# Converting the second MoE's weights two pieces a step, with four more pieces converted in the first MoE's last two steps

## The chip, the cores and the metric

One NeuronCore of a Trainium2 chip runs the whole program. The metric is the device time of one execution in microseconds (us). Engine names are those of the profile: PE is TensorE's matmul, PEld its weight load, DVE is VectorE, ACT is ScalarE, POOL is GpSimd, SP is SyncE, whose queue issues the DMAs.

## The reference

Three layers follow each other, all in float32.

```
attention: 4 batches x 8 heads, 512 local tokens (window of 32 each side) and 32 global ones, head size 64
x    = attention output, rearranged to (2304 tokens, 512)
MoE1: h = x @ w_in (512x1024); s = h * softmax(h); ln = (s - mean) / sqrt(var + 1e-6) * g_ln; x = ln @ w_out (1024x512)
MoE2: h = x @ w_in (512x2048); g = h where h >= 1, 0 where h <= -1, else (h + 1)^2 / 4; out = g @ w_out (2048x512)
```

Weights reach the kernel as 64-bit words (float64 numbers), so every weight has to be turned into float32 on the chip before a matmul can use it.

## The kernel before, in words

**Precision.** Each float32 operand is held as a pair (hi, lo) of fp32r tiles: `split` (L124) lets ACT copy the value to hi, and DVE or POOL subtracts hi from it to give lo. A product is three matmuls (hi by hi, hi by lo, lo by hi), written by `mm3` (L175).

**Weights.** A piece is a [128, 512] block of weights, 512 KB as 64-bit words. `fetch` (L159) issues its DMA into a raw buffer, and `convert` (L129) makes hi and lo of it: ACT takes the absolute value of the high words (L137), DVE does four passes (clamp L139, shift L143, sign L145, low bits L147), and `split` writes hi (ACT) and lo (DVE or POOL). A pair of pieces goes through these passes side by side. The raw buffers (tag `wraw`) are three and the working tiles (tag `w32`) are three. A raw buffer comes free when L147 has read its low words, and only then does SP issue the next load into it; `weights(n)` (L167) converts the next n pieces, and the `fetch` behind it tops the prefetched pieces up to three.

**Pieces and stages.** Sixteen pieces belong to MoE1. `CONV` and the first four entries of `STEP` (1, 2, 3, 2) use them up, so the list of pieces to do is empty from then until entry 12. The 32 pieces of MoE2 come in the order of `order2` (L449): for each 128 columns f of the 2048, its w_in piece ("i", f) and, two later, its w_out piece ("o", f). Counted from 0, piece 2f - 2 is thus ("i", f) for f from 2 on, and piece 2f + 3 is ("o", f) for f up to 13.

MoE1 runs in 17 steps p, one for each tile of 128 tokens (L597). A step multiplies tile p by w_in (`b1`), then does a layer-norm chain on DVE, ACT and POOL, transposes the tile of the step before (`b3`), and multiplies by w_out (`b4`). From step 12 on each step converts `STEP[p]` pieces of MoE2: 1, 2, 2, 1, 1, seven in all, with POOL doing the lo subtraction.

MoE2 runs over three blocks of tokens b (6, 6 and 5 tiles) and, within a block, over the 16 column groups f, one "step" of the loop at L660 each. A step converts pieces (with DVE doing the lo subtraction), multiplies the block by w_in of group f in two halves (`h2`, PE's `h`), and accumulates group f - 2 of the output in two parts (`accum`, PE's `acc`): first half of h, three tiles of acc, second half of h, three tiles of acc. Behind each half, DVE clamps the PSUM result (L504), ACT squares it (L505), DVE takes the maximum (L506), which frees the PSUM bank, and `split` writes g. The PSUM pool `psA` has three banks; in the blocks of six tiles one of them is an accumulator, so the two halves of h have one bank each, and half 0 of the next step needs the bank that half 0 of this step used. In steps 1 to 17 of the loop the remaining 25 pieces are converted, 2 in a step with odd f and 1 in a step with even f.

**Order.** PE and SP execute in the order written. On DVE, ACT and POOL a scheduler orders the instructions by a simulated timeline; each engine then executes in that fixed order. With `vec.gate` set (it is in MoE2) one rule is added at L140: the first DVE pass of a conversion stands behind the last DVE instruction written before it, which is the maximum of the second half of the step before. When block b ends, `ysplit` (L485) splits the input of block b + 1 into the same `yT` tiles.

Of the kernel before, what the change touches and what calls it, by code (L numbers as in the profile page):

```python
# [55 lines left out]
ORDER_1 = "h3x0421g5w"  # L56

CONV = [2, 2, 1, 3]
STEP = [1, 2, 3, 2, 5, 3, 3, 4, 4, 3, 2, 2, 1, 2, 2, 1, 1]

WARM_S = [12, 4, 3, 4, 3]
WARM_P = [2, 5]
# [6 lines left out]
def kernel(ctx, tc, qk, vwin, qkg, vloc, vglo, w1i, w1o, g_ln, w2i, w2o, out):  # L69
# [51 lines left out]
    vec = Ordered()  # L121
# [7 lines left out]
    def convert(weights, eng=nc.gpsimd):  # L129

        ws = []
        for (hi, lo), raw, scale in weights:
            t = stg.tile([P, 512], I32, tag="w32", name="w32")
            words = raw.rearrange("p (n two) -> p n two", two=2)
            ws.append((hi, lo, words[:, :, 0], words[:, :, 1], t, t.bitcast(F32), scale))
        for hi, lo, low, high, t, tf, scale in ws:
            act(out=tf, in_=high.bitcast(F32), func=AF.Abs)  # L137
        for hi, lo, low, high, t, tf, scale in ws:
            first = nc.vector.tensor_scalar(tf, tf, WORD_LO, WORD_HI, ALU.max, ALU.min)  # L139
            if vec.gate and vec.last is not None:  # L140
                tc.add_manual_dep(first.ins, vec.last.ins.name, mybir.DependencyInfo(mybir.DependencyClass.NoSync, mybir.DependencyReason.DATA), reason="order")
        for hi, lo, low, high, t, tf, scale in ws:
            nc.vector.tensor_scalar(t, t, 3, 0x3FFFFFF8, ALU.logical_shift_left, ALU.bitwise_and)  # L143
        for hi, lo, low, high, t, tf, scale in ws:
            nc.vector.scalar_tensor_tensor(out=t, in0=high, scalar=-0x40000000, in1=t, op0=ALU.bitwise_and, op1=ALU.bitwise_or)  # L145
        for hi, lo, low, high, t, tf, scale in ws:
            nc.vector.scalar_tensor_tensor(out=t, in0=low, scalar=29, in1=t, op0=ALU.logical_shift_right, op1=ALU.bitwise_or)  # L147
        for hi, lo, low, high, t, tf, scale in ws:
            t3 = tf.rearrange("p (k n) -> p k n", k=hi.shape[1])
            if scale is not None:  # L150
                nc.gpsimd.tensor_tensor(out=t3, in0=t3, in1=scale.unsqueeze(2).to_broadcast(list(t3.shape)), op=ALU.mult)
            split(hi, lo, t3, eng)
# [6 lines left out]
    def fetch(n=1):  # L159
        n = max(0, n)  # L160
        for make, src, scale in todo[:n]:
            raw = rooms.pop(0) if rooms else stg.tile([P, 1024], I32, tag="wraw", name="wraw")
            dma(out=raw, in_=src)
            fetched.append((make, raw, scale))
        del todo[:n]

    def weights(n=1, eng=nc.gpsimd):  # L167
        while n > 0:
            m = min(n, 2)
            fetch(max(0, m - len(fetched)))  # L170
            convert([(make(), raw, scale) for make, raw, scale in fetched[:m]], eng)
            del fetched[:m]
            n -= m
# [311 lines left out]
    def ysplit(b):  # L485
        n = xy[b].shape[2]
        yT[b] = [(yTr[0][:, k, :n], yTr[1][:, k, :n]) for k in range(KD)]
        for k in range(KD):
            split(*yT[b][k], xy[b][:, k])

    def h2(b, f, half):

        n = xy[b].shape[2] // 2
        sl = slice(n * half, n * half + n)
        s = sring[(b * K2 + f) % len(sring)][:, sl]
        if half == 0:
            gt[b, f] = gring[(b * K2 + f) % len(gring)]
        gh, gl = (a[:, sl] for a in gt[b, f])
        ps = psA.tile([P, 512], F32, tag="A", name="h2")[:, :n]
        w = w2["i", f]  # L500
        for k in range(KD):
            mm3(ps, [((w[0][:, k], w[1][:, k]), [y[:, sl] for y in yT[b][k]])], k == 0, k == KD - 1)

        vec.tensor_scalar(s, ps, -1.0, 1.0, ALU.max, ALU.min)  # L504
        act(out=s, in_=s, func=AF.Square, bias=0.5, scale=0.5)  # L505
        tt(out=s, in0=ps, in1=s, op=ALU.max)  # L506
        split(gh, gl, s, vec if b == len(BLOCKS) - 1 and f >= K2 - 2 else nc.gpsimd)

    def accum(b, f, tiles):
        nt = len(BLOCKS[b])  # L510
        if b not in accs:
            a0, a1 = (psH.tile([P, 2, 512], F32, tag="H", name="acc") for _ in range(2))
            accs[b] = [a0[:, 0], a0[:, 1], a1[:, 0], a1[:, 1], psY.tile([P, 512], F32, tag="Y", name="acc4")]
            if nt == 6:
                accs[b].append(psA.tile([P, 512], F32, tag="A", name="acc5"))
        gh, gl = gt[b, f]
        w = w2["o", f]
        for i in tiles:
            sl = slice(P * i, P * i + P)
            mm3(accs[b][i], [((gh[:, sl], gl[:, sl]), (w[0][:, 0], w[1][:, 0]))], f == 0, f == K2 - 1)  # L520

    def finish(b, i):
        a = accs[b][i]
        t = BLOCKS[b][i]
        if i < 4:
            o = stg.tile([P, DM], I32, tag="w32", name="o").bitcast(F32)
        else:
            o = stg.tile([P, 1024], I32, tag="wraw", name="o2").bitcast(F32)[:, :DM]
        if i % 2:
            vec.tensor_copy(o, a)  # L530
        else:
            act(out=o, in_=a, func=AF.Copy)
        if t < NL:
            r = SB * (t // NB) + SG + P * (t % NB)
            dma(out=out[r:r + P, :], in_=o)
        else:
            for c in range(B):
                dma(out=out[SB * c:SB * c + SG, :], in_=o[32 * c:32 * c + 32])

    with tc.manual_schedule(engines={mybir.EngineType.PE, mybir.EngineType.SP}):  # L540
# [56 lines left out]
        for p in range(NT):  # L597
            t = p + LEAD
            vec.gate = p < 3
            order, n = (ORDER_0 if p < 3 else ORDER_1), STEP[min(p, len(STEP) - 1)]  # L600
            for i, c in enumerate(order):
# [58 lines left out]
        for i, (b, f) in enumerate(steps):  # L660
            if i == 0:
                continue
            weights(2 if f % 2 else 1, vec)
            fetch(3 + len(rooms) - len(fetched))
            pb, pf = steps[i - 2]
            h2(b, f, 0)
            if i >= 2:
                accum(pb, pf, range(3))
            h2(b, f, 1)
            if i >= 2:  # L670
                accum(pb, pf, range(3, len(BLOCKS[pb])))
            if i >= 2 and pf == K2 - 1:
                for j in range(len(BLOCKS[pb])):
                    finish(pb, j)
            if f == K2 - 1 and b + 1 < len(BLOCKS):
                ysplit(b + 1)
# [77 lines left out]
```

## Time and profile before

| | us |
|---|---|
| median of 3 runs (lowest, highest) | 741.76 (740.01, 744.32) |
| the profiled execution | 742.66 |
| its span, first to last instruction | 740.9 |
| PE busy | 697.9 (94%) |
| PEld busy | 612.7 (83%) |
| DVE busy | 411.8 (56%) |
| ACT busy | 311.4 (42%) |
| POOL busy | 173.1 (23%) |

The profiled execution lies 0.9 us above the median. Busy times are of one execution. An engine's idle time is put down to the instruction whose end it waited for last. MoE1 ends near 327 us, block 0 of MoE2 ends near 472 us, block 1 near 614 us.

### The profile page before, as it was taken

To read this page: it belongs to the slowest core of one execution; us is meant where nothing else is said; L and a number is where in the kernel's file an instruction comes from. 1 tells how busy PE (TensorE), PEld (TensorE's weight loads), DVE (VectorE), ACT (ScalarE), POOL (GpSimd) and SP (SyncE) were. 2 spreads that over 40 slices of the span, in tenths; PEclk is the share of its full clock that TensorE was granted. 3 is DMA by queue.
4 is the path that set the end of the run, shared out by engine and by line. 5 is a ranking of instruction groups with operands and counts; after the bars stand their busy time and mean duration, and the time that the engine had idled before them with its cause. 6 is when DMAs were issued, how large, how long until landed. Compare 5 with 4: busy or idle time off the path is not lost.

```text
span 740.9 us, 14997 instructions
## 1 busy us (share of the span) xinstructions
PE 697.9 (94%) x6265; PEld 612.7 (83%) x6265; DVE 411.8 (56%) x741; ACT 311.4 (42%) x775; POOL 173.1 (23%) x191
## 2 busy tenths in 40 slices
PE   8688999999999999999999966899999999999996
PEld 4466788889899888899888855689989998999995
DVE  3977996555555498629867756543222224322232
ACT  5885854465453355324444433322222224222221
POOL 3233363011101143003222221112222222222210
PEclk9989999999999999999999988799999999999999
DMA  9796653434130232002332221010000000100002
GB/s 344 292 359 247 214 215 119 158 107 163 61 123 1 84 121 86 2 1 86 118 107 89 85 87 48 10 71 15 1 1 0 1 1 28 58 1 1 1 1 71
DMA packets 16341, 66.24 MB, mean 89 GB/s; under 512 B 2193, under 2 KB 3217, under 8 KB 13713
## 3 DMA queue, kind: packets, MB, share of 16 engines
q1 hardware_dynamic: 16272, 65.29, 24.6%
q8 instruction: 49, 0.80, 0.4%
q14 instruction: 20, 0.16, 0.1%
HBM read 60.56 MB, written 4.46 MB: 88 GB/s over the span
## 4 chain that ended last, share of the span: by engine, by line
PE 61%; DVE 16%; DMA 6%; ACT 4%; issue 3%; POOL 1%; SPq 0%; ACTq 0%; DVEq 0%
PE h L180 26%; PE acc L180 19%; PE yT L180 8%; DVE w L145 3%; DMA wraw<-in_w2i_dram 3%; DVE w L147 2%; DMA wraw<-in_w2o_dram 2%; DVE xy L116 2%; DVE w L139 2%; PE plnT L408 2%; DVE w L143 1%; ACT w L137 1%; PE o L309 1%; DVE e L116 1%; PE S L257 1%
## 5 line engine op out<-in xcount | busy, mean ns | idle before, releaser
L180 PE MATMUL h<-yT,w2i 128*128 128x384 f32 (+1 forms) x936 | 169.8, 331 | 5.4 <-ACT w2i L126 4.4
L180 PEld LDWEIGHTS h<-yT,w2i 128*128 128x128 f32 x936 | 160.2, 190 | 13.5 <-ACT w2i L126 4.8
L127 POOL TENSOR_TENSOR g<-xy,g 128x384 fp32r<-128x384 f32 (+1 forms) x92 | 92.6, 1007 | 311.6 <-ACT g L126 283.8
L180 PE MATMUL acc<-w2o,g 128*128 128x512 f32 x510 | 130.6, 399 | 7.6 <-ACT w2o L126 7.1
L116 DVE TENSOR_SCALAR xy<-h 128x384 f32<-128x384 f32 (+1 forms) x96 | 51.1, 532 | 154.6 <-PE h L180 136.3
L180 PEld LDWEIGHTS acc<-w2o,g 128*128 128x128 f32 x510 | 95.4, 190 | 26.4 <-ACT w2o L126 7.8
L505 ACT ACTIVATE xy<-xy 128x384 f32<-128x384 f32 (+1 forms) x96 | 48.3, 503 | 146.4 <-DVE xy L116 146.4
L180 PE MATMUL h<-win,x 128*128 128x512 f32 x408 | 99.8, 399 | 2.1 <-issue 1.2
L180 PE MATMUL yT<-lnT,wout 128*128 128x256 f32 x768 | 95.0, 281 | 1.3 <-DVE lnT L116 0.8
L180 PEld LDWEIGHTS yT<-lnT,wout 128*128 128x128 f32 x768 | 92.0, 188 | 2.6 <-DVE lnT L116 1.0
L180 PEld LDWEIGHTS h<-win,x 128*128 128x128 f32 x408 | 75.5, 188 | 19.6 <-issue 1.4
L116 DVE TENSOR_TENSOR xy<-h,xy 128x384 f32<-128x384 f32 (+1 forms) x96 | 51.2, 533 | 56.6 <-ACT xy L505 56.5
L126 ACT ACTIVATE g<-xy 128x384 fp32r<-128x384 f32 (+1 forms) x96 | 48.7, 507 | 60.7 <-DVE xy L116 41.5
L269 ACT ACTIVATE e<-S,nm 128x128 f32<-128x128 f32 x128 | 45.1, 390 | 20.2 <-DVE nm L116 19.9
L137 ACT ACTIVATE w<-wraw 128x512 f32<-128x512 f32 x45 | 30.5, 681 | 42.7 <-DMA wraw<-in_w2o_dram 20.3
L127 POOL TENSOR_TENSOR x<-xy,x 128x512 fp32r<-128x512 f32 x17 | 23.3, 1369 | 86.5 <-ACT x L126 86.4
L180 PE MATMUL h<-yT,lnT 128*128 128x384 f32 (+1 forms) x216 | 38.8, 328 | 0.0
L180 PE MATMUL acc<-lnT,g 128*128 128x512 f32 x153 | 38.2, 393 | 0.0
L180 PEld LDWEIGHTS h<-yT,lnT 128*128 128x128 f32 x216 | 36.5, 188 | 1.8 <-DVE xy L116 0.3
L145 DVE SCALAR_TENSOR_TENSOR w<-wraw,w 128x512 int32<-128x512 int32 x45 | 35.8, 808 | 0.3
L180 PE MATMUL acc<-w_raw,g 128*128 128x512 f32 x102 | 28.1, 420 | 6.5 <-ACT w_raw L126 4.9
L147 DVE SCALAR_TENSOR_TENSOR w<-wraw,w 128x512 int32<-128x512 int32 x45 | 34.0, 762 | 0.3
(113 smaller groups left out, 829.1 us busy)
## 6 DMA issues: line engine op xcount, KB each, us to landing
vw<-in_vwin_dram SPq DMA_DIRECT2D x16, 1024.0 KB, 5.8
qkT<-in_qk_dram SPq DMA_DIRECT2D x16, 832.0 KB, 7.0
wraw<-in_w2i_dram SPq DMA_DIRECT2D x16, 512.0 KB, 3.6
wraw<-in_w2o_dram SPq DMA_DIRECT2D x16, 512.0 KB, 3.6
wraw<-in_w1o_dram SPq DMA_DIRECT2D x8, 512.0 KB, 4.5
vn<-in_vloc_dram SPq DMA_DIRECT2D x4, 1024.0 KB, 8.5
out_dram<-o SPq DMA_DIRECT2D x16, 256.0 KB, 2.1
wraw<-in_w1i_dram SPq DMA_DIRECT2D x5, 512.0 KB, 11.0
```

The costliest lines, as they stand in the source:

```text
L116: self.last = getattr(nc.vector, name)(*args, **kw)
L126: act(out=hi, in_=src, func=AF.Copy)
L127: eng.tensor_tensor(out=lo, in0=src, in1=hi.bitcast(F32), op=ALU.subtract)
L137: act(out=tf, in_=high.bitcast(F32), func=AF.Abs)
L139: first = nc.vector.tensor_scalar(tf, tf, WORD_LO, WORD_HI, ALU.max, ALU.min)
L143: nc.vector.tensor_scalar(t, t, 3, 0x3FFFFFF8, ALU.logical_shift_left, ALU.bitwise_and)
L145: nc.vector.scalar_tensor_tensor(out=t, in0=high, scalar=-0x40000000, in1=t, op0=ALU.bitwise_and, op1=ALU.bitwise_or)
L147: nc.vector.scalar_tensor_tensor(out=t, in0=low, scalar=29, in1=t, op0=ALU.logical_shift_right, op1=ALU.bitwise_or)
L180: mm(out=dst, lhsT=pairs[i][0][x], rhs=pairs[i][1][y], start=start and j == 0, stop=stop and j == 3 * n - 1)
L269: act(out=e[:, h], in_=Sh[:, h], func=AF.Exp, bias=nm[:, h:h + 1], scale=SCALE, accum_out=rs[t][:, h:h + 1])
L408: nc.tensor.transpose(ps[:, k], ln[t][:, P * c:P * c + P], ident)
L505: act(out=s, in_=s, func=AF.Square, bias=0.5, scale=0.5)
```

## The change

Two places change. In MoE2 every step converts two pieces till none is left. In MoE1 the last two steps convert three pieces each and not one; the zeros stand where the list of pieces is empty, so no instruction hangs on them.

```diff
 CONV = [2, 2, 1, 3]
-STEP = [1, 2, 3, 2, 5, 3, 3, 4, 4, 3, 2, 2, 1, 2, 2, 1, 1]
+STEP = [1, 2, 3, 2, 0, 0, 0, 0, 0, 0, 0, 0, 1, 2, 2, 3, 3]
...
             if i == 0:
                 continue
-            weights(2 if f % 2 else 1, vec)
+            weights(2, vec)
             fetch(3 + len(rooms) - len(fetched))
```

Of MoE2's pieces, 11 are then converted in MoE1 (7 before) and 21 in MoE2: two in each of steps 1 to 10 and one in step 11 (before: 25, in steps 1 to 17).

## Rows read from the trace of the kernel before

**Rows 1.** The page's second part: busy tenths of PE and the granted clock in 40 slices of the span, 18.5 us each.

```profile
PE   8688999999999999999999966899999999999996
PEclk9989999999999999999999988799999999999999
```

**Rows 2.** Busy time in three stretches of MoE2 that begin and end with the same kind of matmul (start:end, length, then busy us and count of PE, PEld, DVE, ACT, POOL; granted clock, DMA share, GB/s).

```profile
339.62:420.94 81.32, 80.29 (x401) 71.65 (x399) 65.11 (x116) 37.06 (x69) 21.49 (x19) 1.00 0.29 100
420.94:493.06 72.12, 55.09 (x231) 46.57 (x232) 41.45 (x69) 25.39 (x45) 13.77 (x13) 0.86 0.15 49
493.06:576.95 83.89, 83.89 (x422) 76.02 (x421) 24.22 (x43) 21.70 (x43) 19.50 (x20) 1.00 0.05 19
```

**Rows 3.** What PE waited for between 421 and 494 us: total, times, longest.

```profile
PE acc L180 <- ACT w2o L126: 7.1, 2, 5.8
PE acc L180 <- ACT w_raw L126: 4.9, 2, 3.5
PE h L180 <- ACT w2i L126: 4.4, 1, 4.4
```

**Rows 4.** PE's timeline in MoE2: start, length, what, count, and in brackets the idle time before it.

```profile
339.62 2.27 PE L180 MATMUL h<-yT,w2i 128*128 128x384 f32 x12
...
420.94 2.35 PE L180 MATMUL h<-yT,w2i 128*128 128x384 f32 x12 [0.64 <-DVE xy L116]
...
437.40 0.80 PE L180 MATMUL acc<-w2o,g 128*128 128x512 f32 x1 [5.75 <-ACT w2o L126]
...
461.31 4.30 PE L180 MATMUL h<-yT,w2i 128*128 128x384 f32 x12 [4.38 <-ACT w2i L126]
...
477.75 4.52 PE L180 MATMUL acc<-w_raw,g 128*128 128x512 f32 x9 [3.52 <-ACT w_raw L126]
...
490.38 0.49 PE L180 MATMUL acc<-w_raw,g 128*128 128x512 f32 x1 [1.35 <-ACT w_raw L126]
...
493.06 2.24 PE L180 MATMUL h<-yT,w2i 128*128 128x384 f32 x12
```

**Rows 5.** The chain that ended last, in the steady part of block 1: the second half of h in one step, and the same ten steps later.

```profile
493.23 2.08 PE h L180 x12
...
576.95 2.08 PE h L180 x12
```

**Rows 6.** The same chain inside block 0, from 374 to 423 us: start, length, what (w is the conversion's working tile, wraw the raw buffer, xy the evaluation of h).

```profile
374.83 3.64 DMA wraw<-in_w2i_dram
378.56 0.67 ACT w L137
379.23 0.42 ACT xy L505
379.68 0.56 DVE xy L116
380.24 0.67 DVE w L139 x2
...
387.86 0.66 ACT w L137
...
395.46 0.67 ACT w L137
...
404.78 0.67 ACT w L137
...
413.11 0.66 ACT w L137
...
422.53 0.66 ACT w L137
```

**Rows 7.** The timelines of ACT, DVE and PE in block 0, one line each, in order of time: the first load that lands in MoE2 as ACT takes it up, the maximum of a first half, and the matmul that needed its bank.

```profile
342.26 0.67 ACT L137 ACTIVATE w<-wraw 128x512 f32<-128x512 f32 x1 [1.53 <-DMA wraw<-in_w2i_dram]
...
385.79 0.54 DVE L116 TENSOR_TENSOR xy<-h,xy 128x384 f32<-128x384 f32 x1
...
386.39 2.38 PE L180 MATMUL h<-yT,w2i 128*128 128x384 f32 x12
```

**Rows 8.** PE's timeline where block 1 gives way to block 2.

```profile
612.28 2.24 PE L180 MATMUL acc<-w_last,g 128*128 128x512 f32 x9
614.36 1.92 PE L180 MATMUL h<-yT,w2i 128*128 128x320 f32 x12
```

**Rows 9.** Busy time in the last two full steps of MoE1 (columns as in rows 2).

```profile
282.81:294.94 12.13, 12.13 (x83) 11.04 (x82) 9.99 (x18) 7.33 (x14) 3.10 (x3) 1.00 0.26 88
294.94:307.00 12.06, 12.06 (x82) 10.95 (x81) 10.21 (x16) 5.64 (x11) 0.55 (x1) 1.00 0.00 1
```

**Rows 10.** The timelines of PE and DVE at the end of MoE1, in order of time: the transposes of a tile two steps before the end, the last layer-norm multiply, the transposes that use it, and DVE's first work of MoE2 (in brackets the idle time before each).

```profile
281.96 1.09 PE L408 MATMUL plnT<-ident,e 128*128 128x128 f32 x8 [0.63 <-DVE e L116]
...
311.12 0.81 DVE L116 TENSOR_SCALAR e<-e,mv,rstd 128x1024 f32<-128x1024 f32 x1 [0.73 <-POOL rstd L397]
...
314.49 1.04 PE L408 MATMUL plnT<-ident,e 128*128 128x128 f32 x8
...
328.97 0.56 DVE L116 TENSOR_SCALAR xy<-h 128x384 f32<-128x384 f32 x1 [11.88 <-PE h L180]
```

**Rows 11.** One conversion pass over the whole span: its durations in ns (min/median/max).

```profile
L143 DVE TENSOR_SCALAR w<-w x48: 373/421/1515, 11.1 to 487.0; 128x512 int32<-128x512 int32 x48
```

**Rows 12.** Busy time and granted clock around three of PE's waits (columns as in rows 2).

```profile
446.00:452.60 6.60, 5.01 (x24) 3.92 (x24) 4.70 (x8) 2.09 (x4) 1.87 (x2) 1.00 0.26 79
456.00:466.00 10.00, 5.62 (x18) 4.78 (x18) 6.68 (x12) 2.49 (x5) 1.14 (x1) 0.66 0.16 52
484.00:495.00 11.00, 9.41 (x47) 8.05 (x47) 6.34 (x10) 3.22 (x6) 2.03 (x2) 1.00 0.08 30
```

## The prediction

> **What bounds the kernel now.** I read the slices of the span first, then the stretches of MoE2, then PE's waits, PE's timeline, and the chain that ended last. In the slices the reader is to see one hole: PE is busy 9 tenths or more nearly everywhere, but falls to 6 in slices 24 to 26 (425 to 480 us), and the granted clock falls there too [rows 1].
>
> The steady step gives the measure of the hole. In block 1, where no weights are converted, the same matmul group comes back after ten steps at 576.95 - 493.23 = 83.72 us, 8.372 us a step [rows 5]. From the second half of h of step 2 (339.62) to that of step 17 (493.06) lie 15 steps, 125.58 us at that pace; they took 153.44 [rows 4]. So 27.86 us are lost there: 1.79 in the first 9.5 steps (81.32 - 79.53) and 26.07 in the last 5.5 (72.12 - 46.05) [rows 2].
>
> The waits name the cause of the 26.07: acc and h wait for the hi copies of weights, 7.1 + 4.9 + 4.4 = 16.4 us [rows 3]. The rest is mostly slow matmuls behind the long waits: twelve matmuls of h took 4.30 us after an idle 4.38, against 2.27 elsewhere, and nine of acc took 4.52 after an idle 3.52 [rows 4]. In the stretch the mean granted clock is 0.86, so part of it ran at 1.2 and not 2.4 GHz [rows 2]. Counting pieces gives the reason: step i needs pieces up to 2i - 1. By the end of step 12 there are 7 + 18 = 25 converted (0 to 24), and step 13 needs piece 25, which is converted in step 13 itself, and so on to step 17.
>
> The 1.79 us of the earlier stretch have another cause, which matters more for the change. There the chain runs round a loop outside PE: a load of 3.64 us into a freed raw buffer; ACT's absolute value of it (378.56); behind that on ACT the square of h's second half (379.23); DVE's maximum (379.68); behind the maximum, by the gate, the conversion passes (380.24); and the last pass frees the next raw buffer. A round with a pair took 387.86 - 378.56 = 9.30, 404.78 - 395.46 = 9.32 and 422.53 - 413.11 = 9.42 us; a round with a single piece 7.60 and 8.33 [rows 6]. A pair and a single make 16.9 to 17.8 us, against 16.74 for two PE steps: the loop already just binds. The matmul group at 386.39 starts right behind the maximum that frees its bank (385.79 + 0.54) [rows 7].
>
> **The change part by part.**
>
> *Weights ready.* Before step i, 11 + 2(i - 1) = 2i + 9 pieces are converted, and 2i are needed. Nine pieces, 4.5 steps, are in hand up to step 11, so even a loop that lags by 14 us leaves no matmul waiting for a weight. The 27.86 us go whole, the slow clock with the waits. What is late next at the end of block 0 is the split of the input for block 1, which lay among conversions before; at the end of block 1, where no conversion is near, acc at 612.28 for 2.24 us leads to h at 614.36 without a gap [rows 8]. I cost it at nothing: the acc group hides it. Term: -27.86.
>
> *A pair in every step of 1 to 10.* DVE has room: without conversions it is busy 24.22 us in ten steps, 2.42 each; in the first stretch 65.11 us over 81.32 / 8.372 = 9.71 steps, less 23.5, leaves 41.6 for some 15 pieces, 2.77 each [rows 2]. A pair step is then 2.42 + 5.54 = 7.96 of 8.372. The loop has no room. Each step now has a pair's round of 9.30 to 9.42, and the raw buffer that the first piece of a pair frees takes the second piece of the next pair, so every round holds one load. The first load of MoE2 is taken up at 342.26 [rows 7]; in the changed kernel that is the second piece of step 2. Eight rounds later, for step 10, it is 342.26 + 8 x 9.33 = 416.9. From that point to the freed bank of half 0 is 386.33 - 378.56 = 7.77 [rows 6, 7], so step 11's h starts at 424.7. Without stalls it would start 8.5 steps after 339.62, at 410.8: a loss of 13.9. If ACT takes the square ahead of the load, the round is shorter by what lies between load and clamp beyond the load's own ACT pass (380.24 - 378.56 - 0.67 = 1.01), 8.3 us, no longer than PE's step, and the loss is 13.9 - 9 x 1.0, about 5; with early rounds overlapped, 2. In all five rounds shown the load is ahead of the square, so I stay near that end, but let the first two rounds be short, since PE does not yet wait at their start: 13.9 - 2 = +11.9. Bounds 2 and 16, the latter for eight rounds at 9.42 (14.6) and a pass or two held up besides. The end of the rounds at step 11 costs nothing: nothing is loaded any more.
>
> *Four more pieces in MoE1.* They bring 16 passes on DVE, 8 on ACT, 4 on POOL and 4 loads, at 2.2 us of DVE each (four of the five passes that make 2.77, since POOL does the subtraction): 8.9 us. DVE is idle 2.1 + 1.9 us in the last two full steps [rows 9]. The last layer-norm multiply ends at 311.93 and its transposes start at 314.49, a slack of 2.56; afterwards DVE has 11.88 us idle ahead of MoE2's first work [rows 10]. If all four are done ahead of the last layer-norm chain, PE waits 8.9 - 4.0 - 2.56 = 2.3 us; if two fall behind it, nothing. Nothing is removed there, so there is no gain. The one wait of transposes on DVE two steps before, where DVE was full of conversions, was 0.63 [rows 10]. I take +1.0, bounds 0 and 7: the upper end lets each of the four wait 1.1 us beside POOL, since the shift pass took 0.42 us at the median and 1.52 at most [rows 11], 2.3 + 4.4 = 6.7. The loads cross no other DMA there, and SP has nothing behind them that is due.
>
> The Trainium skill ("GPSIMD Engine Reference", section 1, Specifications) says that GpSimd's access to SBUF is shared with VectorE, which speaks against the four subtractions on POOL. By it the term would lie at its upper end, 7 and not 1; the spread of the shift pass [rows 11] agrees with it, though not for how often.
>
> *Sum.* On the profiled execution: 742.66 - 27.86 + 11.9 + 1.0 = 727.7 us. That execution lies 0.9 above the median, so I predict 726.8.
>
> **The rivals.**
>
> *The loop does not bind* (ACT's order puts the square ahead of the load, 5 or less lost): 741.76 - 27.86 + 5 + 1 = about 720, down to 716. For it: another set of conversions gives the scheduler another timeline. Against: every round shown has the other order.
>
> *Small waits pull the clock down, slower than before.* With a round of 9.33, PE idles about 1 us in each of some nine steps. If each of these idles halves the clock for a group, as the long ones did (4.30 against 2.08 to 2.27, about 2.1 us each time [rows 4, 5]), that adds ten times 2.1: 741.76 - 27.86 + 11.9 + 1.0 + 21 = 748. It ends slower once more than eight groups are hit. For it: the clock did fall behind idles of 3.5 us and more, 0.66 in the stretch around 461 [rows 12]. Against: around the idles of 1.4 us at 449 and 490 the clock is 1.00 [rows 12], as it is over the whole first stretch with its shorter waits [rows 2].
> The Trainium skill ("TensorE: Matmul & The Clock Gate", section "A second HAM failure mode: psum-queue depth-cycling") tells of a kernel whose matmul groups went round PSUM banks with small idles in between, and whose clock swung between its two levels. By it this rival would be the forecast, 748; the traces so far do not bear it out.
>
> *MoE1's end grows long.* If the added passes delay the last chain by 5 to 8 us, PE idles over 3.5 us there and a slow group follows: 731 to 736. For it: ready conversions are put in early, between the links of the chain. Against: DVE's idle in rows 9.
>
> *It does not do what it says*, because the added MoE1 conversions are not done in time and the waits stay: 741.8. For it: nothing in the count of pieces.
>
> **How the numbers follow.** Forecast (722 to 731) 0.62; loop not binding 0.20; MoE1's end 0.09; clock 0.05; no effect 0.04. The range takes the bounds of the two unknown terms: low 741.76 - 27.86 + 2 + 0 = 716, high 741.76 - 27.86 + 16 + 7 = 737. Within 0.5% (3.7 us) is what a measurement of this kernel can't tell from no change. Faster: 0.62 + 0.20 + 0.09 = 0.91; same 0.04; slower 0.05.
>
> **What would show it right or wrong.** Right: no wait of PE for a hi copy of weights in MoE2; the granted clock 1.00 from 340 us on; no gap at the end of block 0; in block 0 waits of h for DVE's maximum, near 1 us a step, 10 to 12 us in all until step 11; rounds of load, absolute value, square, maximum of 9.3 us. Wrong: a step of 8.37 all through block 0 (the loop did not bind), PE waits of more than 2 us between 283 and 327, or slow matmuls behind short waits.

## The result

The changed kernel takes 723.04 us (median of 4 runs, 721.82 to 723.34), the kernel before 740.88 us (4 runs): a ratio of 0.975, with a 95% interval of 0.9712 to 0.9788. The profiled execution took 723.34 us with a span of 721.5, against 742.66 and 740.9.

The page's slices (18.0 us each) show the hole of [rows 1] filled.

```profile
PE   8778899999999999899999999999999999999996
PEclk8999999999999999999999999999999999999999
```

The next views answer to [rows 2]: the same two stretches of MoE2, from the second half of h of step 2 to h of step 12 and on to step 17 (columns as there). They took 84.98 and 45.96 us, against 81.32 and 72.12. At 8.372 us a step they would take 79.53 and 46.05, so the first loses 5.45 (1.79 before) and the second nothing (26.07 before): 22.5 us won. Of the 5.45, 3.84 are idle time of PE; the rest is busy time, 81.14 us for work that takes 79.53 at the steady pace.

```profile
342.75:427.73 84.98, 81.14 (x401) 71.47 (x399) 76.80 (x138) 42.56 (x78) 25.17 (x20) 1.00 0.34 112
427.73:473.69 45.96, 45.96 (x232) 41.59 (x231) 15.91 (x27) 14.98 (x27) 11.57 (x12) 1.00 0.00 1
```

All that PE waits for between 340 and 480 us is one line (total, times, longest); the waits for hi copies of [rows 3] are gone.

```profile
PE h L180 <- DVE xy L116: 3.8, 5, 1.1
```

At the end of block 0 acc leads into block 1's first h without a gap, as [rows 8] had it for the next block. PE's timeline:

```profile
459.06 2.24 PE L180 MATMUL acc<-w_last,g 128*128 128x512 f32 x9
461.13 2.27 PE L180 MATMUL h<-yT,w2i 128*128 128x384 f32 x12
```

Some 3 us are given back earlier. From the first product with w_in of MoE1's step 13 (257.7 in both) to MoE2's first h it is 72.11 us (257.70 to 329.81), against 68.97 (257.72 to 326.69). PE's timeline there, and then its clock over the second and third of these lines:

```profile
289.63 5.11 PE L180 MATMUL yT<-lnT,wout 128*128 128x256 f32 x40 [0.89 <-DVE lnT L116]
296.62 1.80 PE L408 MATMUL plnT<-ident,e 128*128 128x128 f32 x8 [1.88 <-DVE s L116]
298.07 6.83 PE L180 MATMUL h<-win,x 128*128 128x512 f32 x24
```

```profile
296.62:304.74 8.12, 8.12 (x33) 6.82 (x34) 7.30 (x12) 4.76 (x8) 4.58 (x3) 0.79 0.56 196
```

The idle time is 0.89 + 1.88 and 0.30 later, 3.07 us against 0.63 + 0.31 + 0.81 = 1.75 before. The rest is slow work behind the 1.88: 1.80 for eight transposes that take 1.04 elsewhere in the same timeline, 6.83 for 24 products that take 5.84, 1.75 us together. In this execution the 1.32 and the 1.75 make the 3.1; e8 below shows the same kernel with as late an end and no slow clock. On DVE conversion passes (w) stand between the links of the layer-norm chain of step 14's tile (mv, rstd, e), and its last multiply comes just ahead of these transposes:

```profile
291.95 0.20 DVE L116 BATCH_NORM_AGGREGATE mv<-st 128x2 f32<-128x12 f32 x1
292.07 0.37 DVE L143 TENSOR_SCALAR w<-w 128x512 int32<-128x512 int32 x1
...
293.83 0.14 DVE L116 TENSOR_SCALAR rstd<-mv 128x1 f32<-128x1 f32 x1
293.89 0.41 DVE L139 TENSOR_SCALAR w<-w 128x512 f32<-128x512 f32 x1
294.22 1.28 DVE L145 SCALAR_TENSOR_TENSOR w<-wraw,w 128x512 int32<-128x512 int32 x2
295.43 0.41 DVE L143 TENSOR_SCALAR w<-w 128x512 int32<-128x512 int32 x1
295.76 0.80 DVE L116 TENSOR_SCALAR e<-e,mv,rstd 128x1024 f32<-128x1024 f32 x1
```

From the start of step 15's h to these transposes DVE runs 16 passes that write or read w, 8.50 us, and in the kernel before 3, 1.88 us (instructions on w only: DVE, ACT, POOL; the first line is of the changed kernel, the second of the kernel before):

```profile
281.96:296.62 14.66, 8.50 (x16) 4.37 (x7) 4.51 (x3) 1.00 0.32 109
282.81:294.15 11.34, 1.88 (x3) 2.88 (x5) 2.55 (x2) 1.00 0.28 94
```

So -22.5 + 3.1 = -19.4, the change of the span.

In the chain that ended last the rounds of [rows 6] can be read again, in steps 7 to 10:

```profile
383.69 0.66 ACT w L137
384.35 0.42 ACT xy L505
384.79 0.56 DVE xy L116
385.35 0.67 DVE w L139 x2
...
389.38 3.59 DMA wraw<-in_w2i_dram
...
393.05 0.66 ACT w L137
...
402.85 0.67 ACT w L137
...
412.63 0.68 ACT w L137
```

These three rounds took 9.36, 9.80 and 9.78 us. The first load in MoE2 is taken up at 345.46, so the five rounds up to 383.69 took 7.65 on the mean. ACT's timeline shows how the two kinds differ: in the rounds of the early kind the square of the second half (L505) stands ahead of the absolute value (L137) of the load that begins the round, in the late kind behind it.

```profile
366.46 0.51 ACT L505 ACTIVATE xy<-xy 128x384 f32<-128x384 f32 x1
368.88 0.68 ACT L137 ACTIVATE w<-wraw 128x512 f32<-128x512 f32 x1 [1.91 <-DMA wraw<-in_w2i_dram]
...
393.05 0.66 ACT L137 ACTIVATE w<-wraw 128x512 f32<-128x512 f32 x1 [2.02 <-DMA wraw<-in_w2i_dram]
393.61 0.51 ACT L505 ACTIVATE xy<-xy 128x384 f32<-128x384 f32 x1
```

### The profile page after: what moved, and what is told of

The parts are those of the page before. It is cut to its first block, busy times and chain, and to the rows that moved or that the text cites. A ratio compares the mean times of both kernels' runs of the same rounds, so it can differ in the third digit from the quotient of the medians.

```text
span 721.5 us, 14998 instructions
## 1 busy us (share of the span) xinstructions
PE 691.1 (96%) x6265; PEld 607.2 (84%) x6265; DVE 405.5 (56%) x737; ACT 311.8 (43%) x775; POOL 184.3 (26%) x195
## 4 chain that ended last, share of the span: by engine, by line
PE 65%; DVE 14%; DMA 4%; ACT 3%; issue 3%; POOL 2%; SPq 0%; ACTq 0%; DVEq 0%
PE h L180 28%; PE acc L180 21%; PE yT L180 8%; DMA wraw<-in_w2i_dram 4%; DVE w L145 3%; DVE w L147 2%; PE plnT L408 2%; DVE xy L116 2%; DVE w L139 1%; PE o L309 1%; DVE w L143 1%; DVE nm L116 1%; ACT w L137 1%; DVE e L116 1%; PE S L257 1%
## 5 line engine op out<-in xcount | busy, mean ns | idle before, releaser
L180 PE MATMUL h<-yT,w2i 128*128 128x384 f32 (+1 forms) x936 | 167.2, 327 | 1.2 <-DVE xy L116 1.2
L127 POOL TENSOR_TENSOR g<-xy,g 128x384 fp32r<-128x384 f32 (+1 forms) x92 | 94.9, 1032 | 285.5 <-ACT g L126 254.6
L180 PEld LDWEIGHTS h<-yT,w2i 128*128 128x128 f32 x936 | 157.9, 188 | 8.5 <-DVE xy L116 2.4
L180 PE MATMUL acc<-w2o,g 128*128 128x512 f32 x510 | 127.9, 394 | 0.0
L505 ACT ACTIVATE xy<-xy 128x384 f32<-128x384 f32 (+1 forms) x96 | 48.5, 505 | 166.2 <-DVE xy L116 166.2
L137 ACT ACTIVATE w<-wraw 128x512 f32<-128x512 f32 x45 | 30.6, 683 | 39.7 <-DMA wraw<-in_w2i_dram 16.7
L145 DVE SCALAR_TENSOR_TENSOR w<-wraw,w 128x512 int32<-128x512 int32 x45 | 37.5, 843 | 0.1
L147 DVE SCALAR_TENSOR_TENSOR w<-wraw,w 128x512 int32<-128x512 int32 x45 | 34.8, 784 | 0.1
L180 PEld LDWEIGHTS acc<-lnT,g 128*128 128x128 f32 x153 | 28.3, 188 | 5.1
```

The lines of the kernel that those rows point to most:

```text
L127: eng.tensor_tensor(out=lo, in0=src, in1=hi.bitcast(F32), op=ALU.subtract)
L180: mm(out=dst, lhsT=pairs[i][0][x], rhs=pairs[i][1][y], start=start and j == 0, stop=stop and j == 3 * n - 1)
```

## The experiments

Two measures are taken from each run's profile: "MoE1's end", the 68.97 and 72.11 us above, and "block 0's loss", 1.79 + 26.07 = 27.9 us before and 5.4 in the changed kernel. The kernel before took 743.59 us beside e1 to e4, 744.1 beside e5 to e8 and 743.28 beside e9.

| run | median us | ratio to before, 95% | MoE1's end | block 0's loss |
|---|---|---|---|---|
| e1 pairs in MoE2 alone | 720.85 | 0.9698 (0.9664 to 0.9733) | 68.2 | 6.7 |
| e2 four more in MoE1 alone | 720.98 | 0.9695 (0.9665 to 0.9724) | 72.7 | 4.2 |
| e3 square first | 719.62 | 0.9673 (0.9643 to 0.9702) | 71.4 | 2.4 |
| e4 four behind MoE1 | 718.89 | 0.9671 (0.9641 to 0.9700) | 69.0 | 5.9 |
| e5 no loads | 719.26 | 0.9667 (0.9643 to 0.9691) | 72.2 | 1.9 |
| e6 e4 and e3 | 718.43 | 0.9662 (0.9638 to 0.9686) | 69.1 | 4.8 |
| e7 e6 at 2 and 1 | 713.16 | 0.9593 (0.9568 to 0.9619) | 68.2 | 0.3 |
| e8 the change again | 722.74 | 0.9728 (0.9699 to 0.9757) | 72.3 | 4.7 |
| e9 e7 without the order | 718.41 | 0.9666 (0.9626 to 0.9707) | 69.0 | 4.3 |

The measures are of one execution; executions differ by up to 2.5 us in where MoE1's step 12 begins (240.4 to 242.9 us), far ahead of the change, so the stages tell more than the medians. The loss of the changed kernel itself came out at 5.4 and, in e8, at 4.7, so a difference of under 1 us between two losses is within what two executions show.

**e1: one half of the change.** The entries for steps 4 to 11 meet an empty list; only the last two matter. Diff from the changed kernel:

```diff
-STEP = [1, 2, 3, 2, 0, 0, 0, 0, 0, 0, 0, 0, 1, 2, 2, 3, 3]
+STEP = [1, 2, 3, 2, 5, 3, 3, 4, 4, 3, 2, 2, 1, 2, 2, 1, 1]
```

> Two conversions a step in MoE2, but MoE1 as before (7 pieces there, 25 left). Theory: the 3.1 us by which MoE2 starts later in the changed kernel come from the four added pieces, so they go; the loop of raw buffers runs two rounds more, at up to 1.4 us each, so block 0 loses 5 to 8 us and not 5.5. Time 720 to 723. If the later start were only another order of DVE's work and not the added passes, MoE2 would start as late as in the changed kernel and the time would be 723 to 726. If two pieces a step alone did not cure the waits for weights, over 730.

MoE1's end is 68.2 us and block 0's loss 6.7: as the theory has it, the added pieces make the later start. Pairs alone cure the waits for weights: this is all that PE waits for between 345 and 490 us.

```profile
PE h L180 <- DVE xy L116: 4.6, 6, 1.2
```

**e2: the other half.** The rate in MoE2 is that of the kernel before. Diff from the changed kernel:

```diff
-            weights(2, vec)
+            weights(2 if f % 2 else 1, vec)
```

> Four more pieces in MoE1, but 2 and 1 by turns in MoE2. Theory: 11 pieces of lead are enough for 1.5 a step (step 13 needs 26 and has 29), so all waits for weights go as well; pairs alternate with singles, a round of 16.9 to 17.7 us for two steps of 16.74, so block 0 loses 2 to 3 us and not 5.5; MoE1's 3.1 us stay. Time 719 to 721. Rival: the rate of two a step is what cures the waits; then waits for hi copies remain in steps 14 to 17 and the time is 730 or more.

The lead of four pieces alone also cures them: either half does. The loss of 4.2 is above the 2 to 3 expected; PE's only waits in MoE2 are for the maximum, up to 0.8 us each, in every second step to the end of the conversions:

```profile
PE h L180 <- DVE xy L116: 3.0, 5, 0.8
```

In MoE1 the clock fell again, here behind an idle 1.77; PE's timeline (40 such products take 5.11 us in the changed kernel) and the clock over it:

```profile
289.12 6.51 PE L180 MATMUL yT<-lnT,wout 128*128 128x256 f32 x40 [1.77 <-DVE lnT L116]
```

```profile
289.12:295.63 6.51, 6.50 (x40) 6.30 (x40) 6.51 (x15) 2.46 (x4) 1.95 (x2) 0.74 0.27 83
```

**e3: the square ahead of the load.** Diff from the changed kernel:

```diff
-            act(out=tf, in_=high.bitcast(F32), func=AF.Abs)
+            a = act(out=tf, in_=high.bitcast(F32), func=AF.Abs)
+            if squares:
+                tc.add_manual_dep(a.ins, squares[-1].ins.name, mybir.DependencyInfo(mybir.DependencyClass.NoSync, mybir.DependencyReason.DATA), reason="order")
...
-        act(out=s, in_=s, func=AF.Square, bias=0.5, scale=0.5)
+        q = act(out=s, in_=s, func=AF.Square, bias=0.5, scale=0.5)
+        if half == 1 and f >= 2:
+            squares.append(q)
```

> The changed kernel with one order added on ACT: from step 3 of MoE2 on, the absolute value of a new load stands behind the square of the second half of the step before. Theory: the 5.5 us lost in block 0 come from rounds in which the square waits behind a load (9.4 to 9.8 us in steps 7 to 10); with the square ahead a round is about 8.4 and the loss falls to 0 to 2 us: time 718 to 720. Rival: DVE itself is full with a pair each step (76.8 of 85 us busy), the order on ACT is nothing, and the loss stays near 5.5: 722 to 724. A third: the absolute value now comes too late and holds DVE up, a loss over 8: 726 or more.

The loss falls to 2.4 us, from 5.4 in the changed kernel's profile (4.7 in e8). So the order on ACT made 2.3 to 3 of them. What stays, somewhat above the 2 allowed, lies in steps with DVE nearly full; the stretch to step 12 (columns as in rows 2) has DVE busy 79.86 of 82.02 us:

```profile
341.75:423.77 82.02, 80.84 (x400) 71.65 (x399) 79.86 (x137) 41.58 (x77) 22.48 (x19) 1.00 0.37 116
```

**e5: no loads.** `fetch` takes the raw buffer of the last piece fetched ahead of MoE2's loop, and no load is issued any more. Diff from the changed kernel:

```diff
+            if resident:
+                raw = resident[0]
+            else:
...
+        resident.append(fetched[-1][1])
```

> The changed kernel without the loads in MoE2: the pieces not yet fetched when MoE2's loop begins are all converted from one raw buffer that is already on the chip, so 18 loads and the wait for a free raw buffer are left out and most of MoE2 uses wrong weights. All DVE, ACT and POOL work stays. Theory: without a load in the loop nothing holds the square back, DVE's 8.0 us fit into a step of 8.37, and block 0 loses 0 to 1.5 us and not 5.5. Rival: DVE's load alone makes the loss, which stays at 4 us or more. Time 717 to 721 by the theory, with the 3 us of MoE1 still in it.

The loss is 1.9, little above the theory's 1.5, and its DMA share in this stretch is 0.00. Loads make 3.5 us of the 5.4 (2.8 of e8's 4.7). The 1.9 that stay are DVE's: from one step's h to the next it is 9.27 us at step 4 and 9.17 at step 7, and at most 8.47 at all others, and around both of the late starts, where PE waits 0.74 and 0.58 us for the maximum, DVE is busy without a gap (11.20 of 11.20 us and 5.00 of 5.00 in the second and third line). One pass there, the clamp (L139) at 359.61, took 1.24 us and not 0.41 while a subtraction ran on POOL from 359.47 to 360.56; POOL's share in the 1.9 was not tried.

```profile
342.47:423.98 81.51, 80.19 (x400) 71.48 (x399) 77.91 (x138) 42.52 (x78) 22.82 (x20) 1.00 0.00 1
353.00:364.20 11.20, 10.57 (x52) 9.04 (x50) 11.20 (x22) 6.34 (x11) 2.79 (x2) 1.00 0.00 0
386.00:391.00 5.00, 4.42 (x23) 3.68 (x22) 5.00 (x10) 2.84 (x6) 0.05 (x2) 1.00 0.00 2
```

**e4: the four extra pieces behind MoE1's products**, with `STEP` as in e1. Diff from the changed kernel:

```diff
         b4(NL // 2 - 1, 1)
+        vec.gate = True
+        weights(4)
+        fetch(3 + len(rooms) - len(fetched))
```

> The four extra pieces are converted behind MoE1's last products (b4) and not in its last two steps, with the order rule on; DVE is idle for some 11.9 us there. MoE2 as in the changed kernel. Theory: the 3.1 us of MoE1 go and block 0 loses 5 to 6 as now: time 719 to 721. Rival: the passes end too late, MoE2's first steps wait for them and what is won is lost there: 722 to 725.

MoE1's end is 69.0 us, as before the change, and the loss 5.9: the idle time of DVE took the four pieces at no cost that shows. The time, 718.89, is just below the 719 to 721 expected.

**e6: e4 and e3 together.**

> The extra four pieces behind MoE1's last products and the order on ACT (square ahead of the next loads' absolute values) together. Theory: the two costs are separate and their cures add up: from MoE1's step 13 to MoE2 69.0 us (72.1 in the changed kernel), loss of block 0 about 2.5 us (5.5 there), time 715 to 718. If the two were one cost seen twice, 719 to 721.

Half a miss. MoE1's end adds up (69.1), the loss doesn't: 4.8 and not 2.5, and the time, 718.43, is just above the 715 to 718 expected. The loss lies mainly in steps 4 and 6 (9.54 and 9.95 us from one step's h to the next), not in 9 and 10 (8.46 and 8.55), and DVE is busy 81.33 of 84.37 us:

```profile
339.57:423.94 84.37, 81.43 (x401) 71.36 (x400) 81.33 (x139) 42.14 (x78) 23.25 (x19) 1.00 0.35 113
```

So in this pair of runs, e4 and e6, the order on ACT is worth 1.1 us of loss and not 3. Why it is worth less here than in e3, with DVE as full, was not tried and is not shown.

**e7: the same at 2 and 1 pieces a step** (the edit of e2 added).

> As the kernel before this one in the list, but with 2 and 1 pieces a step by turns. Theory: singles give each round room, so block 0 loses 1 to 2 us; steps 12 to 14 still convert, at nearly no cost; time 714 to 717. Rival: the later conversions reach the end of block 0 and cost there what is won before: 717 to 719.

Better than all expected: the loss is 0.3 us, every step from step 3 on is between 8.32 and 8.45, and DVE has 9.5 us of room in the stretch. This is the fastest kernel, 713.16 us against 722.74 for the changed one beside it.

```profile
337.67:417.63 79.96, 79.79 (x401) 71.96 (x399) 70.43 (x120) 37.80 (x72) 21.52 (x20) 1.00 0.35 110
```

**e8: the changed kernel again.**

> The changed kernel itself on the chip of these runs, to stand beside them. All theories: 0.973 to 0.979 of the kernel before, MoE1's end 72.1 us, block 0's loss 5.5 us.

Its ratio, 0.9728, lies at the lower end of what was expected, MoE1's end is 72.3, and the loss 4.7, not 5.5. At MoE1's end the profile differs from the first one: the idles are 2.02 and 1.88 us, and the granted clock behind both is 1.00.

```profile
289.35 5.11 PE L180 MATMUL yT<-lnT,wout 128*128 128x256 f32 x40 [2.02 <-DVE lnT L116]
296.33 1.09 PE L408 MATMUL plnT<-ident,e 128*128 128x128 f32 x8 [1.88 <-DVE s L116]
```

```profile
289.35:294.46 5.11, 5.10 (x40) 4.83 (x40) 5.11 (x12) 2.38 (x5) 1.95 (x2) 1.00 0.33 106
296.33:303.02 6.69, 6.69 (x34) 5.61 (x35) 6.69 (x11) 4.09 (x7) 4.59 (x3) 1.00 0.66 236
```

So this end is as late as the first without any slow matmul. The same stage of e5 (72.2) has idles of 1.77 and 1.88 us and that of e3 (71.4) of 0.99 and 1.89, both at a granted clock of 1.00 as well.

**e9: e7 without the order on ACT.**

> Four pieces behind MoE1's last products, 2 and 1 pieces a step by turns, without the added order on ACT: it tells how much of the best kernel so far (713.2 us, block 0 losing 0.3 us) is the rate and how much the order. Theory: without the order the square again waits behind loads in each pair's round and block 0 loses 3 to 4.5 us, as it did with this rate before (4.2): time 716 to 718, 0.963 to 0.966 of the kernel before. Rival: the rate alone gives the rounds room enough, the loss is under 1.5 and the time 713 to 715.

The loss is 4.3, and another 1.0 us is lost in steps 0 to 2; the time is 0.4 above the range expected. DVE has no less room than in e7 (16.3 us), but the stretch is 2.8 us longer:

```profile
338.19:420.93 82.74, 80.68 (x400) 71.38 (x398) 66.44 (x117) 37.51 (x70) 21.63 (x19) 1.00 0.29 98
```

At this rate the order is worth 5.2 us of time (718.41 to 713.16), while with pairs in every step (e4 to e6) it brought 0.5. The lower rate without the order brought as little (718.89 in e4, 718.41 here): with the four pieces behind MoE1 neither helps much alone, and the two together do.

A fourth raw buffer, which would take the load out of the round in another way, was not tried, for want of room.

## Why the prediction was right, and where it was off

The time was forecast as 727.7 us for the profiled execution and came out at 723.34; 726.8 against a median of 723.04, within the range. Part of that is luck. Two of the three terms were off, in opposite directions, by 6.5 too much and 2.1 too little; with the first of these two alone put right the forecast would have been 720.3, below the range and where the first rival had it.

*Weights ready, -27.86.* Right. No wait for a hi copy is left in MoE2, the slow clock of that stretch went with the waits, the last 5.5 steps run at 45.96 (46.05 at the steady pace). The split for block 1 costs nothing, as costed. e2 shows that four pieces of lead would have been enough without the faster rate, and e1 that the rate would have been enough without the lead.

*A pair in every step, +11.9.* The mechanism holds in part of the rounds, and the size was twice too large: 5.4, with waits of h for the maximum of 3.8 us in all and not 10 to 12. The step that failed is "in all five rounds shown the load is ahead of the square, so I stay near that end, but let the first two rounds be short". Five of the eight rounds were short, 7.65 us on the mean, and there the square stood ahead; only three were long, at 9.4 to 9.8, a little above the 9.30 to 9.42 taken from rows 6. The order of a scheduler in another set of steps was read from five rounds as if it were fixed. Against the 5.4, e3 and e5 put what the load ahead of the square costs at 3.0 and 3.5 us (2.3 and 2.8 against e8's 4.7). What stays, 1.9 without any load, is DVE's own, which I had at nothing with 7.96 us of 8.372: without slack to speak of, the maximum comes late in steps where DVE has fallen behind.

*Four more pieces in MoE1, +1.0.* Mis-sized, 3.1, within the bounds of 0 to 7. I looked for the cost at the last layer-norm chain; it fell two tiles earlier, on that of step 14, as the scheduler put ready passes between its links, 16 where there had been 3. The slow clock behind the 1.88, which I had counted only behind idles of 3.5 us, is 1.75 of the 3.1 in the first profile, but not the cause of the late end: in e8 and e5 the end is as late with none. One of the signs that were to show the prediction wrong, slow matmuls behind a short wait, came here and not in block 0. e1 and e4 show that it is the place of the pieces that costs: without them, or behind the products, the stage takes 68.2 and 69.0. No run separated what POOL's share in it is. In the chain of step 14 one pass is drawn out, the sign pass (L145) at 285.52, which took 1.66 us where others take 0.68, while POOL subtracted from 285.14 to 288.35; if POOL is the reason, that is about 1 us.

*The rivals.* The loop that does not bind was half true: its order held in five rounds of eight, and the loss of 5.4 lies nearer to its 5 than to the 11.9. The clock rival fell in MoE2: with waits of h up to 1.13 us the granted clock stays 1.00 over the whole stretch, and in e1, with waits up to 1.2, the slices of block 0 stand at 9 tenths or more. So for this kernel the rule of the Trainium skill ("TensorE: Matmul & The Clock Gate", section "A second HAM failure mode: psum-queue depth-cycling") is not borne out at waits of this size. MoE1's end grew, but by 3 and not by 5 to 8.

## What to carry to other kernels

Count what each step needs against what is ready: a lead built up in idle time can serve as well as a higher rate, and leaves the engines room (e2, e7). Where a wait for a transfer stands on an engine ahead of the work that frees a buffer, try the freeing work ahead of it: here that took the loss from 5.4 to 2.4 us (e3), and from 4.3 to 0.3 where DVE also had room (e9 to e7). Room without that order, or the order without room, brought about half a microsecond (e9 and e6 against e4). Extra work goes where the engine's timeline has a real hole, behind the last products here, and not into the last steps of a full stage.

## What was not expected of the hardware

The granted clock fell behind idles of PE of 1.88 us (0.79 over the next 8 us) and, in e2, of 1.77 us (0.74 over 6.5 us). In the kernel before, only idles of 3.5 us and more had shown a fall; behind the 1.36 and 1.35 us of [rows 12] the clock stayed at 1.00. But the length of an idle does not settle it: it also stayed at 1.00 behind 2.02 and 1.88 us in e8, the same kernel, behind 1.77 and 1.88 in e5 and behind 1.89 in e3. Why it fell in two of these five executions and not in the others stays open.
